# Scores in plain float32 in the quarters of the array, keys in blocks of 128, and eps added on ScalarE

## The chip, the core and the metric

The kernel runs on one core of a Trainium2 chip. TensorE (PE) multiplies; its weight loads have a row of their own in the profile (PEld). VectorE (DVE), ScalarE (ACT) and GpSimd (POOL) do the elementwise work, SyncE (SP) and POOL issue most transfers. The metric is the device time of one execution in microseconds (us).

## The reference

Attention with mixing over heads before and after the softmax, then two gated feed-forward layers, all in float32:

```python
scores = scale * np.matmul(q, k.transpose(0, 1, 3, 2))      # 2 batches, 12 heads, 448 x 448
scores = np.einsum('bhij,hg->bgij', scores, w_pre)
scores = scores - np.max(scores, axis=-1, keepdims=True)
attn = np.exp(scores)
attn = attn / (np.sum(attn, axis=-1, keepdims=True) + 1e-09)
attn = np.einsum('bhij,hg->bgij', attn, w_post)
x = np.matmul(attn, v)                                      # head_dim 64; then 896 x 768
x = (x @ w_a) * (x @ w_b) @ w_out                           # 768 -> 1536 -> 768
h = np.maximum(x @ w_in, 0.0)
out = (h * h) @ w_out2                                      # 768 -> 2048 -> 768
```

## The kernel before

The attention goes over eight tiles: batch b of 2, and four tiles t of query rows (120, 120, 120 and 88). A tile is cut into pairs of groups of ten rows: six pairs in a tile of 120, five in the tile of 88, 46 in all. One **slot** of the main loop does the following for one pair, and the order of all engines is fixed by the order of the calls in that loop:

- `premix` (L297): two groups of heads times `w_pre`, four float32 matmuls in the four 64x64 quarters of the array, out of G, the tile of scores with rows and heads on the partitions. Result in two of three PSUM banks "T".
- softmax: `smin` (a minimum on DVE, L306, into nb) and `sexp` (exponential on ACT with its sum, L313) for two halves; then `weights2` on DVE: z plus eps (L325), reciprocal (L326), and w2 = w_post / z (L327).
- `post` (L350): the exponentials e, 64 keys at a time, as stationary operand, and w2 (60 columns) as moving operand. This turns keys onto the partitions. The 448 keys are four blocks of 112, each cut in 64 and 48: 32 float32 matmuls for a pair, in quarters, into two PSUM banks "post" (from slot 38 on, in every other slot, "qk").
- `evac` copies both banks to A, the first on ACT (L377), the second on DVE (L375).
- `qk` (L212): scores of a later tile, for one pair of heads (six such calls for a tile), the heads in the two row halves of the array with up to 120 columns each, into two banks "qk". `qk_copy` takes them out, the even head on ACT (L223), the odd one on DVE (L221), and `spread` sends them by DMA to G (POOL issues for even heads, SP for odd ones). In batch 0, tiles 0 to 2, this is plain float32. From then on q and k are each split in a high and a low float32r part (`split_q`: ACT and six POOL subtractions, L170; `split_k`: ACT and DVE, L176 and L177), and three products are summed.

After the last slot of a tile comes `av` (L389): A times v, for each of six head pairs c four key blocks of 112 by two heads, each head in one column half of the array. The pairs go by two into a bank: c = 0, 1 into "av", c = 2, 3 into one of the two "post" banks, c = 4, 5 into "av" again; `av_out` (L399, DVE) copies each bank to x32. Between these calls stand the softmax of the pair after next, splits of k, and steps that split weights of the layers that follow (`steps`: ACT and DVE). In the text below T0 is the start of a tile's first `av` matmul.

The feed-forward layers follow the attention. They are 2448 float32r matmuls of 128x128 by 448 columns (L642 to L644).

Of the kernel before, what the change touches and what calls it, by code (L numbers as in the profile page):

```python
# [16 lines left out]
DM = H * D  # L17
# [11 lines left out]
JP = 112  # L29
NJ = S // JP  # L30
# [36 lines left out]
def place_mixed(g, k, h):  # L67
    return 64 * g + PK * (k % KG) + h


@with_exitstack
def attention_moe_kernel(
# [61 lines left out]
    kp = {}  # L134
    qp = {}
# [6 lines left out]
    def load_q(b, t, eng=nc.sync, parts=1):  # L142
        x = w_p.tile([128, UW], F32, tag="wc", name="q", bufs=2)
# [12 lines left out]
    def load_k(b, c, eng=nc.sync):  # L156
        if c % 3 == 0:
# [15 lines left out]
    def split_k(b, c):  # L173
        x = kk[b, c]
        hi, lo = single(f"ks{2 * c}"), single(f"ks{2 * c + 1}")
        nc.scalar.copy(hi, x)  # L176
        nc.vector.tensor_tensor(out=lo, in0=x, in1=rd(hi), op=ALU.subtract)  # L177
        kp[b, c] = (hi, lo)

    def split_q(b, t):  # L180
        n = NC * TILE
        x = qq[b, t]
        hi = w_p.tile([128, UW], F32R, tag="wh", name="qh", bufs=3)
        lo = w_p.tile([128, UW], F32R, tag="wl", name="ql", bufs=3)
        nc.scalar.copy(hi[:, 0:n], x[:, 0:n])
        lower(lo[:, 0:n], x[:, 0:n], hi[:, 0:n], 6)
        qp[b, t] = (hi, lo)

    def load_v(b, i, n=1):
        if b not in vv:  # L190
            x = sb.tile([128, NJ * DM], F32, tag="v", name="v", bufs=2)
            vv[b] = x[0:JP].rearrange("p (j d) -> p j d", j=NJ)
        g, j = divmod(i, NJ)
        nc.sync.dma_start(
            out=vv[b][:, j:j + n, g * DM // 2:(g + 1) * DM // 2], in_=v[b, g, j:j + n].rearrange("j p d -> p j d")
        )


    def qk(b, t, c, tags=("qk", "qk")):
# [108 lines left out]
    def sexp(b, m, f):  # L308
# [8 lines left out]
        E[b, m, f] = e  # L317

    def weights2(b, m):
# [5 lines left out]
        nc.vector.tensor_tensor(out=z, in0=z, in1=eps[0:q].to_broadcast([q, 2]), op=ALU.add)  # L325
# [12 lines left out]
    def post(b, m):  # L338
# [17 lines left out]
    def evac(b, m, g):  # L356
        t, r, n = PAIRS[m]
        if r == 0 and g == 0:
            A[b, t] = a_p.tile([JP, NJ * H, TILE], F32, tag="a", name="a")
        if g >= n:  # L360
            return
        src = Pps[b, m][g][0:JP, 0:2 * NJ * H * KG].rearrange("p (f g k) -> p f g k", f=2, k=KG)
# [16 lines left out]

    def av(b, t, c):  # L380
        n = ROWS[t]
        if c % 2 == 0:
            AVp[b, t] = ps("post" if c == 2 else "av")
        p = AVp[b, t]
        o = (c % 2) * TILE
        for j in range(NJ):
            for e in range(2):
                g = 2 * c + e
                nc.tensor.matmul(  # L389
                    p[64 * e:64 * e + 64, o:o + n], vv[b][:, j, g * D:(g + 1) * D], A[b, t][:, j * H + g, 0:n],  # L390
                    start=(j == 0), stop=(j == NJ - 1), skip_group_check=True,
                )

    def av_out(b, t, q):
        n = ROWS[t]
        if t == 0:
            x32[b][q] = xpair(b, q, F32)
        pv = AVp[b, t][:, 0:2 * TILE].rearrange("p (c i) -> p c i", c=2)
        nc.vector.tensor_copy(x32[b][q][:, :, OFFS[t]:OFFS[t] + n], pv[:, :, 0:n])  # L399
# [28 lines left out]
    v0 = sb.tile([128, NJ * DM], F32, tag="v", name="v0", bufs=2)  # L428
# [40 lines left out]
    def load_w(u, i=0, n=1):  # L469
# [20 lines left out]
    SPLITS = (  # L490
        (((0, 0), (0, 1), (0, 2)), (), ((0, 3),)),
        (((0, 4), (0, 5), (1, 0)), (), ((1, 1), (1, 2))),
        (((1, 3),), (), ((1, 4), (1, 5))),
    )
# [23 lines left out]
    for i in range(NJ):  # L518
        at(mid, 2, load_v, 0, 2 * i, 2)
    for ti, (b, t) in enumerate(tiles):  # L520
        s0, sp = base[ti], span[ti]
        if ti + 1 < len(tiles):
# [12 lines left out]
            if ti + 2 < len(tiles):  # L535
                if ti:
                    d = 3 if ti == 5 else 0
                    at(mid, s0 - 1 - d, load_q, *tiles[ti + 2], nc.sync, 2)
                    if not d:
                        at(mid, s0 + (ti != 3), split_q, *tiles[ti + 2])  # L540
        if ti + 1 < len(tiles):
            sl = s0 + sp - 1
            if ti == 4:
                at(end, sl, split_q, 1, 3)
            for c in range(NC):
                at(end, sl, av, b, t, c)
                if c % 2:
                    work = [(steps, STEPS[b, t][c // 2])] if (b, t) in STEPS else [
                        (split_k, *x) for x in SPLITS[t][c // 2]
                    ]  # L550
                    if c < 5:
                        for x in work:
                            at(end, sl, *x)
# [371 lines left out]
```

## Time and profile before

| | |
|---|---|
| median of 3 runs | 705.17 us (703.37 to 710.95) |
| the profiled execution: time, span | 704.41 us, 702.6 us |
| PE, PEld busy | 682.6 us (97%), 579.0 us (82%) |
| DVE, ACT, POOL busy | 489.1 us, 309.8 us, 67.5 us |
| attention, until the last av ends | 0 to about 204.4 us |
| feed-forward layers | about 204.4 to 702.6 us |

Matmuls are pipelined, and a record's length contains its way through the array. What a block of matmuls costs PE is therefore read from the start of its first record to the start of the next block. A float32 matmul leaves two records. An engine takes its instructions in the program's order, so an instruction that waits holds all that stand behind it.

### The profile page before, as it was taken

What the parts mean: (1) busy time and instruction counts of PE and PEld (TensorE: products, weight loads), DVE (VectorE), ACT (ScalarE), POOL (GpSimd) and SP (SyncE); (2) the same over time, 40 slices, a digit from 0 to 9 for tenths busy, and PEclk for the clock granted to TensorE, in tenths of its full rate; (3) what the DMA queues carried; (4) which work ended last, traced back from release to release, by engine and by line L of the source; (5) the groups of instructions that cost most, each with busy time, mean ns of one, the idle gap of its engine ahead of it and who ended that gap; (6) DMA issues with size and microseconds to landing.
All of it is one profiled execution on the core that took longest, in us unless ns stands there. A gap on an engine that the chain in (4) does not pass through costs nothing.

```text
span 702.6 us, 15964 instructions
## 1 busy us (share of the span) xinstructions
PE 682.6 (97%) x6749; PEld 579.0 (82%) x6749; DVE 489.1 (70%) x839; ACT 309.8 (44%) x580; POOL 67.5 (10%) x129
## 2 busy tenths in 40 slices
PE   9979998999899999999999999999999999999997
PEld 3445666666689999999999999999999999999996
DVE  6848987899865876766767556668888887645530
ACT  3647666777643333433333322335555553323210
POOL 7203331336200000000000000000000000000000
PEclk9989999999999999999999999999999999999999
DMA  7874576644202423332233422422324234343300
GB/s 232 207 194 140 163 193 178 175 121 145 86 3 90 135 90 113 113 124 102 90 121 104 135 90 90 135 90 96 130 90 132 94 96 153 137 147 130 117 28 27
DMA packets 29109, 84.94 MB, mean 121 GB/s; under 512 B 5075, under 2 KB 18478, under 8 KB 29037
## 3 DMA queue, kind: packets, MB, share of 16 engines
q1 hardware_dynamic: 23949, 73.24, 32.4%
q0 software_dynamic: 4224, 9.43, 5.3%
q8 instruction: 53, 0.87, 0.5%
q10 hardware_dynamic: 864, 1.24, 0.5%
q14 instruction: 19, 0.16, 0.1%
HBM read 62.29 MB, written 2.75 MB: 93 GB/s over the span
## 4 chain that ended last, share of the span: by engine, by line
PE 87%; DMA 5%; DVE 3%; issue 3%; ACT 2%; POOL 0%; ACTq 0%; DVEq 0%; POOLq 0%
PE T L642 9%; PE T L644 9%; PE T L643 9%; PE post L644 6%; PE post L643 6%; PE post L642 6%; PE qk L644 6%; PE qk L643 6%; PE qk L642 6%; PE post L350 4%; PE qk L212 4%; PE av L644 3%; PE av L643 3%; PE av L642 3%; PE av L389 3%
## 5 line engine op out<-in xcount | busy, mean ns | idle before, releaser
L604 ACT CAST wh<-wc 128x768 fp32r<-128x768 f32 x68 | 56.8, 835 | 118.2 <-DVE wc L598 104.6
L608 DVE TENSOR_TENSOR wl<-wc,wh 128x768 fp32r<-128x768 f32 x68 | 64.9, 954 | 48.2 <-ACT wh L604 48.1
L313 ACT ACTIVATE e<-T,nb 128x448 f32<-128x448 f32 (+1 forms) x92 | 57.6, 630 | 46.1 <-DVE nb L306 43.4
L644 PE MATMUL T<-m,wl 128*128 128x448 f32 x207 | 75.6, 365 | 0.0
L643 PE MATMUL T<-m,wh 128*128 128x448 f32 x207 | 75.6, 365 | 0.0
L642 PE MATMUL T<-m,wh 128*128 128x448 f32 x207 | 75.6, 365 | 0.0
L586 DVE SCALAR_TENSOR_TENSOR wa<-wr,wa 128x768 uint32<-128x768 uint32 x68 | 65.2, 958 | 2.3
L598 DVE SCALAR_TENSOR_TENSOR wc<-wc,wa 128x768 uint32<-128x768 uint32 x68 | 65.2, 958 | 2.3
L350 PEld LDWEIGHTS post<-w,e 64*48 64x48 f32 (+1 forms) x2624 | 44.0, 129 | 23.1 <-issue 11.1
L581 ACT ACTIVATE wc<-wr 128x768 f32<-128x768 f32 x68 | 61.3, 902 | 0.0
L306 DVE TENSOR_REDUCE nb<-T 128x1 f32<-128x448 f32 (+1 forms) x92 | 52.9, 615 | 7.5 <-PE T L297 6.3
L297 PE MATMUL T<-G,wpre_sb 64*64 64x448 f32 x352 | 49.7, 566 | 6.5 <-DMA G<-x 4.8
L350 PE MATMUL post<-w,e 64*48 64x60 f32 (+1 forms) x2624 | 49.9, 221 | 4.7 <-DVE w L327 2.5
L594 DVE TENSOR_SCALAR wc<-wc 128x768 f32<-128x768 f32 x68 | 38.0, 558 | 19.5 <-ACT wc L581 19.5
L642 PE MATMUL post<-m,wh 128*128 128x448 f32 x125 | 45.7, 365 | 0.0
L644 PE MATMUL post<-m,wl 128*128 128x448 f32 x125 | 45.6, 365 | 0.0
L643 PE MATMUL post<-m,wh 128*128 128x448 f32 x125 | 45.6, 365 | 0.0
L642 PE MATMUL qk<-m,wh 128*128 128x448 f32 x116 | 42.4, 365 | 0.0
L644 PE MATMUL qk<-m,wl 128*128 128x448 f32 x116 | 42.4, 365 | 0.0
L643 PE MATMUL qk<-m,wh 128*128 128x448 f32 x116 | 42.4, 365 | 0.0
L642 PEld LDWEIGHTS T<-m,wh 128*128 128x128 f32 x207 | 38.9, 188 | 3.1
L643 PEld LDWEIGHTS T<-m,wh 128*128 128x128 f32 x207 | 38.9, 188 | 3.1
(179 smaller groups left out, 1441.1 us busy)
## 6 DMA issues: line engine op xcount, KB each, us to landing
wr<-w SPq DMA_DIRECT2D x65, 768.0 KB
G<-s POOLq DMA_DIRECT2D x24, 210.0 KB, 5.2
G<-s SPq DMA_DIRECT2D x20, 210.0 KB
outT<-ta SPq DMA_DIRECT2D x11, 224.0 KB
wr<-w SPq DMA_DIRECT2D x12, 192.0 KB
k<-kT SPq DMA_DIRECT2D x9, 224.0 KB
q<-qT SPq DMA_DIRECT2D x10, 180.0 KB
G<-s POOLq DMA_DIRECT2D x12, 140.0 KB, 3.4
```

What stands on the lines that cost most here:

```text
L297: nc.tensor.matmul(p[f][o:o + 64, 0:S], wpre_sb[i:i + 64, o:o + 64], G[t % 2][i:i + 64, r + g, :], start=True, stop=True, skip_group_check ...
L306: nc.vector.tensor_reduce(out=NB[b, m][0:q, f:f + 1], in_=Tps[b, m][f][0:q, 0:S], op=ALU.min, axis=AX.X)
L313: nc.scalar.activation(out=e[0:q], in_=Tps[b, m][f][0:q, 0:S], func=ACTF.Exp, bias=NB[b, m][0:q, f:f + 1], scale=-1.0, accum_out=Z[b, m][0 ...
L350: nc.tensor.matmul(p[g][x:y, c:c + k], e[o:o + 64, j * JP + x:j * JP + y], w2[o:o + 64, f, :], start=True, stop=True, skip_group_check=True,)
L581: nc.scalar.activation(out=st["c"], in_=rd(st["high"]), func=ACTF.Abs, scale=HSC)
L586: nc.vector.scalar_tensor_tensor(out=a, in0=st["high"], scalar=0x80000000, in1=a, op0=ALU.bitwise_and, op1=ALU.bitwise_or)
L598: nc.vector.scalar_tensor_tensor(out=cu, in0=cu, scalar=3, in1=st["a"], op0=ALU.logical_shift_left, op1=ALU.bitwise_or)
L604: nc.scalar.copy(st["hi"], st["c"])
L608: nc.vector.tensor_tensor(out=lo, in0=st["c"], in1=rd(st["hi"]), op=ALU.subtract)
L642: nc.tensor.matmul(p[:, 0:S], hi[:, sl], x[0], start=first, stop=False)
L643: nc.tensor.matmul(p[:, 0:S], hi[:, sl], x[1], start=False, stop=False)
L644: nc.tensor.matmul(p[:, 0:S], lo[:, sl], x[0], start=False, stop=last)
```

## The change

- `qk`: plain float32 in all tiles. Each head pair is four matmuls in the four quarters: rows of q 0 to 63 and 64 to 119 in the column halves, the two heads in the row halves. `split_q` and `split_k` and their calls go. q gets buffers of its own, and the k of batch 1 goes straight to the tiles that held its parts.
- Keys: three blocks of 128 and a rest of 64. In `post` every stationary block has 64 columns; for the rest, the two column halves take half of the heads each, so their moving operand has 30 columns. Still 32 matmuls for a pair. A has 42 instead of 48 columns of (block, head) for a row; PSUM holds 420 instead of 480 values for a row of `evac`.
- `av`: `av_start` does the rest of 64 keys for all twelve heads, twelve matmuls in quarters, into **two** banks at once ("av" and "post"), which both stay in use to the end of the tile's `av`. Then c goes 0, 1, 4, 2, 3, 5 with three blocks of 128. `av_out` comes twice; each time DVE copies two head pairs (L414) and then ACT the third (L415).
- eps: `sexp` adds it on ACT (L315) behind the second exponential, instead of DVE in `weights2`.

```diff
     def qk(b, t, c, tags=("qk", "qk")):
...
-        if b == 0 and t < 3:
-            parts = [(qq[b, t], kk[b, c])]
-        else:
-            (qh, ql), (kh, kl) = qp[b, t], kp[b, c]
-            parts = [(qh, kh), (qh, kl), (ql, kh)]
-        for i, (x, y) in enumerate(parts):
+        for l, r in ((0, 64), (64, n)):
             for e in range(2):
                 o = 64 * e
                 nc.tensor.matmul(
-                    p[e][0:n, 0:S], x[o:o + 64, c * w:c * w + n], y[o:o + 64, :],
-                    start=(i == 0), stop=(i == len(parts) - 1),
+                    p[e][l:r, 0:S], qq[b, t][o:o + 64, c * w + l:c * w + r], kk[b, c][o:o + 64, :],
+                    start=True, stop=True, skip_group_check=True,
                 )
...
         E[b, m, f] = e
+        if f:
+            z = Z[b, m][0:q]
+            nc.scalar.activation(out=z, in_=z, func=ACTF.Identity, bias=eps[0:q])
...
-        nc.vector.tensor_tensor(out=z, in0=z, in1=eps[0:q].to_broadcast([q, 2]), op=ALU.add)
         nc.vector.reciprocal(out=z, in_=z)
...
-            for j in range(NJ):
+            for j in range(NK + 1):
                 for g in range(n):
                     o = 64 * g
-                    c = (f * NJ + j) * k
-                    for x, y in ((0, 64), (64, JP)):
+                    c = f * NG * KG + j * k
+                    for x in range(2):
+                        y, z, i = (64 * x, 0, k) if j < NK else (0, x * k // 2, k // 2)
                         nc.tensor.matmul(
-                            p[g][x:y, c:c + k], e[o:o + 64, j * JP + x:j * JP + y], w2[o:o + 64, f, :],
+                            p[g][64 * x:64 * x + 64, c:c + i],
+                            e[o:o + 64, j * 128 + y:j * 128 + y + 64], w2[o:o + 64, f, z:z + i],
...
+    def av_start(b, t):
+        n = ROWS[t]
+        AVp[b, t] = [ps(tag) for tag in ("av", "post")]
+        for two in ((0, 2), (1, 3), (4, 5)):
+            for e in range(2):
+                for c in two:
+                    x = 64 * side(2 * c + e)
+                    i, o = PLACE[c]
+                    nc.tensor.matmul(
+                        AVp[b, t][i][64 * e:64 * e + 64, o * TILE:o * TILE + n],
+                        vv[b][x:x + 64, 0, c * D:(c + 1) * D], A[b, t][x:x + 64, NK * H + c, 0:n],
+                        start=(o == 0), stop=False, skip_group_check=True,
+                    )
...
+        nc.vector.tensor_copy(x32[b][i][:, :, o], src[:, :, 0:n])
+        nc.scalar.copy(x32[b][2][:, i, o], p[:, 2 * TILE:2 * TILE + n])
...
-            for c in range(NC):
+            work = [[(steps, k)] for k in STEPS.get((b, t), (0, 0, 0))]
+            at(end, sl, av_start, b, t)
+            for i, c in enumerate(AVC):
                 at(end, sl, av, b, t, c)
...
+                if i == 1:
+                    at(end, sl, *work[0][0])
+                if i == 2:
+                    at(end, sl, av_out, b, t, 0)
+                    at(end, sl, softmax, sl + 2)
+                if i == 4:
+                    at(end, sl, *work[1][0])
+                    at(end, sl, weights2, *plist[sl + 2])
+            at(end, sl, av_out, b, t, 1)
+            at(end, sl, *work[2][0])
```

What moves on the engines is shown at three places. The first is DVE behind the last slot of tile (1, 2), whose `av` starts at 182.88 us in the trace: L399 and L414 are `av_out`, L306 and L301 the two minima of the softmax of the pair after next, L326/L327 and L323/L324 its `weights2`, the others steps on weights. Before:

```order
L327 TENSOR_TENSOR w_3533<-wp,z 128x120 [waits DVE_49]
L582 TENSOR_SCALAR wa<-wr 128x768 [waits DMAHW4_49,DMAHW3_49,DMAHW2_49]
L586 SCALAR_TENSOR_TENSOR wa<-wr,wa 128x768 [waits DVE_49]
L399 COPY x_0_2597<-av 128x2x120 [waits PE_49]
L306 TENSOR_REDUCE nb<-T 128x1 x2
L594 TENSOR_SCALAR wc<-wc 128x768 [waits Activation_49]
L399 COPY x_1_2624<-post 128x2x120 [waits PE_49]
L325 TENSOR_TENSOR z<-z,eps 128x2 [waits Activation_49]
L326 RECIPROCAL z<-z 128x2 [waits DVE_49]
L327 TENSOR_TENSOR w_3595<-wp,z 128x120 [waits DVE_49]
L399 COPY x_2_2647<-av 128x2x120 [waits PE_49]
L598 SCALAR_TENSOR_TENSOR wc<-wc,wa 128x768
```

The same place on DVE in the changed kernel:

```order
L324 TENSOR_TENSOR w_3420<-wp,z 128x120 [waits DVE_49]
L585 TENSOR_SCALAR wa<-wr 128x768 [waits DMAHW3_49,DMAHW2_49,DMAHW1_49]
L589 SCALAR_TENSOR_TENSOR wa<-wr,wa 128x768 [waits DVE_49]
L414 COPY x_0_2516<-av 128x2x120 [waits PE_49]
L301 TENSOR_REDUCE nb<-T 128x1 x2
L597 TENSOR_SCALAR wc<-wc 128x768 [waits Activation_49]
L323 RECIPROCAL z<-z 128x2 [waits Activation_49]
L324 TENSOR_TENSOR w_3492<-wp,z 128x120 [waits DVE_49]
L414 COPY x_1_2517<-post 128x2x120 [waits PE_49]
L601 SCALAR_TENSOR_TENSOR wc<-wc,wa 128x768
```

The copy out of "post" stood ahead of the `weights2` of the pair after next, and now stands behind it. On ACT the same stretch of the changed kernel reads as follows (L308 are the exponentials, L315 eps, L415 the third copy of `av_out`, L376 `evac`):

```order
L415 COPY x_2_2518<-av 128x120 [waits DVE_49]
L308 ACTIVATE e,z<-T,nb 128x448 [waits DVE_49] x2
L315 ACTIVATE z<-z,eps 128x2 [waits Activation_49]
L415 COPY x_2_2518<-post 128x120 [waits DVE_49]
L376 COPY a<-post 128x2x42x5 [waits PE_49]
```

There was no `av_out` on ACT before; each of the two copies waits for the copy that DVE makes of the same bank. The second place is PE behind the same `av`, in the changed kernel:

```order
L400 MATMUL av<-a,v 64x120 x18
L400 MATMUL post<-a,v 64x120 x18
L348 MATMUL post<-w_3420,e 64x60 [waits DVE_49]
L348 MATMUL post<-w_3420,e 64x60
L348 MATMUL post<-w_3420,e 64x60 [waits Activation_49]
```

The third matmul of `post` writes the bank that `av` used, and waits for ACT: for the second L415. (In the other tiles a `qk`, L207, stands between L400 and L348.) The third place is ACT in a slot in the midst of a tile. Before:

```order
L313 ACTIVATE e,z<-T,nb 128x448 [waits DVE_49]
L223 COPY s<-qk 120x448 [waits DMASW0_49,PE_49]
L377 COPY a<-post 112x2x48x5 [waits PE_49]
L185 CAST qh<-q 128x720 [waits DMAHW7_49,DMAHW6_49]
```

The same slot in the changed kernel:

```order
L308 ACTIVATE e,z<-T,nb 128x448 [waits DVE_49] x2
L315 ACTIVATE z<-z,eps 128x2 [waits Activation_49]
L218 COPY s<-qk 120x448 [waits DMASW0_49,PE_49]
L376 COPY a<-post 128x2x42x5 [waits PE_49]
```

The addition of eps stands between the second exponential and the copy that frees a "qk" bank; the cast of q is gone.

## Rows read from the trace of the kernel before

**Rows 1.** Windows; columns: window, length, busy of PE, PEld, DVE, ACT, POOL, PE clock, DMA share, GB/s.

```profile
45.00:200.60 155.60, 146.49 (x3710) 101.84 (x3702) 132.17 (x319) 107.29 (x261) 48.52 (x99) 1.00 0.51 143
204.40:702.60 498.20, 493.97 (x2438) 457.40 (x2436) 326.37 (x458) 182.49 (x272) 0.00 (x0) 1.00 0.31 106
```

**Rows 2.** Timeline, PE, unhindered blocks; columns: start, us, engine, line, operation, tiles, tile, count.

```profile
101.18 0.98 PE L297 MATMUL T<-G,wpre_sb 64*64 64x448 f32 x8
102.09 0.67 PE L212 MATMUL qk<-ks,qh 64*120 64x448 f32 x4
102.89 1.15 PE L350 MATMUL post<-w,e 64*64 64x60 f32 x64
103.87 0.99 PE L297 MATMUL T<-G,wpre_sb 64*64 64x448 f32 x8
```

**Rows 3.** Timeline, PE, a plain float32 qk and the block after it.

```profile
54.87 1.02 PE L212 MATMUL qk<-k,q 64*120 64x448 f32 x4
55.81 1.09 PE L350 MATMUL post<-w,e 64*64 64x60 f32 x62
```

**Rows 4.** Timeline of two slots in tile (1, 0), all engines.

```profile
149.83 1.15 DVE L306 TENSOR_REDUCE nb<-T 128x1 f32<-128x448 f32 x2
...
151.69 0.20 ACT L313 ACTIVATION_READ_ACCUMULATOR e<-T,nb 128x1 f32 x1
151.78 0.53 ACT L223 COPY s<-qk 120x448 f32<-120x448 f32 x1
...
153.13 1.15 PE L350 MATMUL post<-w,e 64*64 64x60 f32 x64
...
154.38 0.69 DVE L375 COPY a<-post 112x480 f32<-112x480 f32 x1
...
154.97 0.14 DVE L325 TENSOR_TENSOR z<-z,eps 128x2 f32<-128x2 f32 x1
...
155.14 0.17 DVE L326 RECIPROCAL z<-z 128x2 f32<-128x2 f32 x1
155.34 0.28 DVE L327 TENSOR_TENSOR w<-wp,z 128x120 f32<-128x120 f32 x1
155.54 0.62 DVE L306 TENSOR_REDUCE nb<-T 128x1 f32<-128x448 f32 x1
```

**Rows 5.** Timeline around the av of tile (0, 2), all engines.

```profile
93.15 1.86 PE L389 MATMUL av<-a,v 112*64 112x120 f32 x32 [0.17 <-DVE a L375]
...
94.81 1.84 PE L389 MATMUL post<-a,v 112*64 112x120 f32 x32
95.05 0.41 DVE L399 COPY x<-av 128x240 f32<-128x240 f32 x1
...
95.37 1.15 DVE L306 TENSOR_REDUCE nb<-T 128x1 f32<-128x448 f32 x2
96.10 0.63 ACT L313 ACTIVATE e<-T,nb 128x448 f32<-128x448 f32 x1 [1.70 <-DVE nb L306]
...
99.02 1.15 PE L350 MATMUL post<-w,e 64*64 64x60 f32 x64
```

**Rows 6.** Timeline around the av of tile (1, 2), all engines.

```profile
182.88 1.86 PE L389 MATMUL av<-a,v 112*64 112x120 f32 x32
...
187.95 1.09 PE L350 MATMUL post<-w,e 64*64 64x60 f32 x62
...
188.84 0.58 PE L297 MATMUL T<-G,wpre_sb 64*64 64x448 f32 x2
...
189.63 0.57 PE L350 MATMUL qk<-w,e 64*48 64x60 f32 x26
...
189.92 0.62 DVE L306 TENSOR_REDUCE nb<-T 128x1 f32<-128x448 f32 x1
```

**Rows 7.** DVE line L325: count, shortest, median and longest in ns.

```profile
L325 DVE TENSOR_TENSOR z<-z,eps x46: 138/152/1247, 17.6 to 197.4; 128x2 f32<-128x2 f32 x44, 64x2 f32<-64x2 f32 x2
```

**Rows 8.** Timeline around 82 us, POOL and DVE.

```profile
81.75 2.43 POOL L170 TENSOR_TENSOR ql<-q,qh 128x120 fp32r<-128x120 f32 x6
...
82.96 1.25 DVE L325 TENSOR_TENSOR z<-z,eps 128x2 f32<-128x2 f32 x1
```

**Rows 9.** Timeline, PE, the longest wait of the start.

```profile
40.36 1.95 PE L297 MATMUL T<-G,wpre_sb 64*64 64x448 f32 x8 [4.58 <-DMA G<-x]
```

**Rows 10.** Groups by form: copies out of PSUM on DVE and ACT; busy us, mean ns, idle before.

```profile
L375 DVE COPY a<-post 112x480 f32<-112x480 f32 x40 | 27.2, 681 | 12.0 <-PE post L350 11.6
L399 DVE COPY x<-av 128x240 f32<-128x240 f32 x12 | 4.8, 401 | 0.0
L371 ACT COPY a<-post 112x240 f32<-112x240 f32 x2 | 0.9, 434 | 2.0 <-PE post L350 2.0
```

More of the change, by code (lines that the diff above doesn't have):

```diff
@@ L28 @@
 GP = 128
-JP = 112
-NJ = S // JP
+NK = S // 128
+KH = S - 128 * NK
+NG = (NK * 2 + 1) * H // 2
+VP = 2 * NK + 1
 NC = DM // 128
@@ L133, in attention_moe_kernel @@
     kw = {}
-    kp = {}
-    qp = {}
     qq = {}
@@ L377, in evac, with av_out @@
             nc.scalar.copy(dst, src)
+    def av_start(b, t):
[11 more added lines that the diff above has]
+                    )
     def av(b, t, c):
         n = ROWS[t]
[L382 to L386, printed above, removed]
+        i, o = PLACE[c]
+        for j in range(NK):
             for e in range(2):
-                g = 2 * c + e
+                h = 2 * c + e
+                g, x = divmod(h, H // 2)
                 nc.tensor.matmul(
-                    p[64 * e:64 * e + 64, o:o + n], vv[b][:, j, g * D:(g + 1) * D], A[b, t][:, j * H + g, 0:n],
-                    start=(j == 0), stop=(j == NJ - 1), skip_group_check=True,
+                    AVp[b, t][i][64 * e:64 * e + 64, o * TILE:o * TILE + n],
+                    vv[b][:, 1 + NK * g + j, x * D:(x + 1) * D], A[b, t][:, j * H + column(h), 0:n],
+                    start=False, stop=(j == NK - 1), skip_group_check=True,
                 )
-    def av_out(b, t, q):
+    def av_out(b, t, i):
         n = ROWS[t]
[L396 to L399, printed above, removed]
+        if t == 0 and i == 0:
+            for q in range(NC // 2):
+                x32[b][q] = xpair(b, q, F32)
+        p = AVp[b, t][i]
+        o = slice(OFFS[t], OFFS[t] + n)
+        src = p[:, 0:2 * TILE].rearrange("p (c i) -> p c i", c=2)
+        nc.vector.tensor_copy(x32[b][i][:, :, o], src[:, :, 0:n])
+        nc.scalar.copy(x32[b][2][:, i, o], p[:, 2 * TILE:2 * TILE + n])
     warm = const.tile([128, 1], F16, name="warm")
@@ L516, in at @@
         d.setdefault(max(slot, 0), []).append(f)
-    for i in range(NJ):
-        at(mid, 2, load_v, 0, 2 * i, 2)
+    for i in range(0, VP, 2):
+        at(mid, 2, load_v, 0, i, 2)
     for ti, (b, t) in enumerate(tiles):
@@ L536, in attention_moe_kernel @@
                 if ti:
[L537 to L540, printed above, removed]
+                    at(mid, s0 - 1, load_q, *tiles[ti + 2], nc.sync, 2)
         if ti + 1 < len(tiles):
             sl = s0 + sp - 1
-            if ti == 4:
-                at(end, sl, split_q, 1, 3)
-            for c in range(NC):
+            work = [[(steps, k)] for k in STEPS.get((b, t), (0, 0, 0))]
+            at(end, sl, av_start, b, t)
+            for i, c in enumerate(AVC):
                 at(end, sl, av, b, t, c)
[L547 to L553, printed above, removed]
-                    at(end, sl, av_out, b, t, c // 2)
-                    if c == 5:
-                        for x in work:
-                            at(end, sl, *x)
-                    elif c == 3:
-                        at(end, sl, weights2, *plist[sl + 2])
-                    else:
-                        at(end, sl, softmax, sl + 2)
+                if i == 1:
[8 more added lines that the diff above has]
+            at(end, sl, *work[2][0])
         if ti == 2:
@@ L688, in attention_tail @@
         last = (B - 1, NTL - 1)
-        for c in range(NC):
+        av_start(*last)
+        for i, c in enumerate(AVC):
             av(*last, c)
-            if c % 2:
-                av_out(*last, c // 2)
+            if i % 3 == 2:
+                av_out(*last, i // 3)
+            if i % 2:
                 steps(1)
@@ L883, in _layout @@
     kT = k.reshape(B, NC, 2, S, D).transpose(0, 1, 2, 4, 3).reshape(B, NC, 128, S)
-    vl = v.reshape(B, 2, H // 2, NJ, JP, D).transpose(0, 1, 3, 4, 2, 5).reshape(B, 2, NJ, JP, DM // 2)
+    vl = np.zeros((B, VP, 128, H // 2, D), f)
+    n = NK * 128
+    vl[:, 1:] = v[:, :, 0:n].reshape(B, 2, H // 2, NK, 128, D).transpose(0, 1, 3, 4, 2, 5).reshape(vl[:, 1:].shape)
+    for h in range(H):
+        o = KH * side(h)
+        vl[:, 0, o:o + KH, h // 2] = v[:, h, n:]
+    vl = vl.reshape(B, VP, 128, DM // 2)
     wpre = np.zeros((128, 256), f)
@@ L890, in _layout @@
             wpre[np.ix_([place(n, h) for h in range(H)], o)] = i["w_pre"]
-            wpost[o, :, n % KG] = i["w_post"]
+            wpost[np.ix_(o, [column(h) for h in range(H)], [n % KG])] = i["w_post"][:, :, None]
         o = 128 + 64 * (n // KG)
```

51 lines of the change are left out of this document (21 added, 30 removed).

## The prediction

> **What bounds the kernel now.** I read the windows first, then the timeline of PE, then all engines over one slot and over one `av`. Behind 204.4 us PE is busy 494.0 of 498.2 us at the full granted clock (1.00 in the row, its 2.4 GHz level) [rows 1]. The change touches nothing there except when that stage starts. So the question is how long the attention takes. Between 45.0 and 200.6 us PE looks busy too, 146.5 of 155.6 us, but a record's length contains waits and the way through the array; block starts tell more.
>
> An unhindered split `qk` costs PE 0.80 us (102.09 to 102.89), a `post` 0.98, a `premix` 0.91 [rows 2]: 2.69 us for a slot. The slots in tile (1, 0) take 2.86 (two of them from 149.83 to 155.54) [rows 4]. What closes that circle is a loop over two slots: from the start of the minima to the start of the ACT copy of the even scores 1.95 us, the copy 0.53 (to 152.31; the "qk" bank is free only then), from there to `post` 0.82, to `evac` 1.25, to z 0.59, to the reciprocal 0.17, w2 0.20, and the next minimum 0.20, in all 5.71 [rows 4]. PE waits about 0.15 us a slot in it. So a gain on PE alone goes into that wait, and what counts is what the change does to this loop and to the `av` stretches.
>
> **The change part by part.**
>
> *A steady slot: 0.* Off the loop comes the addition on DVE, 0.17 (154.97 to 155.14) [rows 4], and in `evac` 60 of 480 columns: by the copies of 480 and 240 columns (681 and 401 ns) [rows 10] 1.17 ns each, 0.07. Onto it comes eps on ACT ahead of the copy that frees the bank. No row shows this operation. Its nearest row is the reading of the accumulator, which takes 0.20 but lets the next start after 0.09 (151.69, 151.78) [rows 4]. As eps waits for that reading to end, I take 0.11 for the wait and 0.11 for itself, 0.22. Bounds are 0.09 in all (no wait seen) and 0.11 + 0.32 = 0.43 (copies of 240 and 448 columns take 0.43 [rows 10] and 0.53 us [rows 4], so a copy of next to none 0.32). `qk` from the free bank to `post` was 0.82. In quarters it is what `premix` costs if the same array shape follows, 0.79 (188.84 to 189.63) [rows 6], plus at most one exposed weight load of about 0.05: 0 to +0.02. Sum -0.02 over two slots: nothing. With the bounds it is -0.07 to +0.1 a slot; some 26 slots run in this loop, so -1.8 to +2.6 us.
>
> *`post`: 0.* Its 64 records in four quarters take 0.98 us, 61 ns each in a quarter [rows 2]. A float32 `av` record of 120 columns takes 104 ns in a half (32 records in 1.66 us, 93.15 to 94.81) [rows 5], so 60 columns alone would take 52. The records with 64 stationary columns are thus held by something other than the columns that stream, and the count of records and their 64 columns stay. Making a quarter of them shorter gains nothing; if columns did count it is 1/8 of 0.8, 0.1 us a pair, half of it in the loop: 0 to -2 us, and I take 0.
>
> *`av` and what stands behind it: +4.9.* On PE: `av_start` is three matmuls in each quarter, 6 records of 104 ns, 0.62, plus about 0.15 for the first load and the change of array shape; the rest 36 records, 3.74. So it ends at T0 + 4.5; before, with `qk` after it, `post` came at T0 + 5.87 (93.15 to 99.02) [rows 5], without at T0 + 5.07 [rows 6]. PE could be at `post` by 5.4, or 4.6.
> But `post` needs both "post" banks, and one is now `av`'s to the end. Its release is the last link of a chain in order on DVE and ACT: c = 0, 1, 4 done at T0 + 0.77 + 1.87, seen by DVE 0.24 later (94.81 to 95.05) [rows 5]: first `av_out` at 2.9; minima 0.32 later, 3.2; exponentials 0.73 after that, 3.95 (95.05, 95.37, 96.10) [rows 5]; to the end of the second sum 1.34 (two starts 0.62 apart, each with its 0.52 and the 0.20 of the reading), 5.3; eps 0.2; reciprocal and w2 0.4, 5.9; second `av_out` 0.40, 6.3; then ACT's copy, which waits for DVE's, 0.3; `post` goes on at about T0 + 6.7. So it starts 0.8 us later than before in the six tiles of which this `post` follows a `qk`, and 1.6 later in tile (1, 2). In the tile of 88 rows PE shrinks with the rows, by 1.33 in the old order, the chain only by 0.7 in its first links: 1.4.
> How much is passed on? Behind 187.95 the next minimum starts 1.97 later [rows 6] and nothing else holds it: T0 + 8.65 against 7.04, all 1.6. Likewise the tile of 88 rows, of which I take 1.3. In the other five DVE comes later than PE today, with splits of k (which go) or steps on weights (which stay) in its queue: 0 to 0.8 each, I take 0.4. Sum 1.6 + 1.3 + 2.0 = 4.9, with bounds 2.5 and 7.
> The tile after which the feed-forward layers follow has no such `post`; there PE's 0.3 is gained in full.
>
> *What goes from POOL and ACT: -1.1.* The addition z + eps took 1247 ns once, against a median of 152 [rows 7], while POOL subtracted for `split_q` [rows 8]; PE's `post` waited for it. Both are gone: -1.1. POOL's 2.4 us for a tile also stood ahead of spreads, and some of the 2.4 may come back: 0 to -2. The casts and splits of k lie in `av` and are in the term above.
>
> *The start: -0.8.* The plain `qk` of batch 0 falls from 0.94 (54.87 to 55.81) [rows 3] to 0.8. But the first tile ends in a wait of 4.58 us for the scores of the next [rows 9], and engines wait there for transfers, so only an earlier issue can help: 0 to -1.5. I take 0.5, and 0.3 for the few plain slots behind that wait. Earlier starts of `av`, by 0.065 for the smaller `evac`, eight times: -0.5.
>
> **Sum** against the profiled execution's 704.4: + 4.9 - 1.1 - 0.8 - 0.5 - 0.3 = 706.6 us, 0.2% above the median of the runs (705.17, itself 0.8 above that execution).
>
> **A rule against the row.** A `premix` followed by `qk` in 64x120 tiles takes 0.91 [rows 2], one followed by a block in its own 64x64 shape 0.79 [rows 6]: 0.12 for the change of shape. The Trainium skill, TensorEngine Tiling (Array Packing), Key Properties, says that changing the tiling mode drains the array; by that rule a slot sheds this drain twice, and the trace agrees. What it would be worth if PE were the bound is the first rival.
>
> **The rivals.**
>
> 1. *PE's gains reach the end.* For: PE is busy at 97% by the page. Per slot with `qk` the premix falls by 0.12 (some 42 of them, 5.0 us), the 12 plain `qk` that follow the first six from 0.94 to 0.8 (1.7), `av` by 0.55 in six tiles and 0.35 in two (4.0): 10.7 in all, and -1.1 from POOL: 692.6. Against: PE waits in the loop of rows 4 already, and the held bank. It would show as slots below 2.7 us.
> 2. *The two row halves take turns in `av_start`* (slower). Both halves write both banks there at once; `premix`, `post` and `qk` keep each row half to a bank, so no row shows it. If they take turns, its 0.62 us doubles, DVE's chain starts 0.6 later, and all of it is passed on in eight tiles: 706.6 + 4.7 = 711.3. It decides the sign by the 1% bound from 0.7 us a tile upward (5.6 over eight tiles). The same page of the Trainium skill, PSUM Pressure, says that different row tiles cannot access the same PSUM bank simultaneously; by that rule this rival holds. No run here shows it so far.
> 3. *The waits behind `av` are absorbed.* If the softmax run ahead covers them, 4.9 becomes 0 to 1 and the time 702 to 703: still within 1%.
>
> **Chances.** Forecast with rival 3: 0.60 (700 to 711). Rival 1, whole or in half: 0.24 (690 to 698). Rival 2 or deeper waits behind `av`: 0.16 (709 to 716). One per cent is 7 us, about what a measurement of this kernel can tell from no change. Faster by over 1% is below 698.1: most of rival 1 and a little of the forecast, 0.24. Slower is above 712.2: half of rival 2 and an edge of the forecast's, 0.13. The rest 0.63. The range is 695.5 to 713: it reaches halfway into rival 1 and over most of rival 2, and holds the bounds above. The forecast's own is 700 to 711.
>
> **What would show each step.** In the changed profile, a slot in tile (1, 0) at 2.8 to 2.9 us, with eps on ACT at 0.1 to 0.25 us; `post` still at 0.98; `qk` plus `premix` without the 0.12; `av` of 4.5 us (5.1 if rows take turns); and behind it PE waiting 1.0 to 2.0 us in `post` for ACT's L415. If that wait is missing, or slots fall below 2.7, the forecast is wrong in that term.

## The result, and the profile after

The changed kernel takes 709.91 us (median of 20 runs, 706.72 to 714.18), the kernel before 703.07 (20 runs beside them, 699.78 to 710.95). The ratio is 1.0103, with a 95% interval of 1.0082 to 1.0123: slower by 1.0%. The forecast was 706.6, no change by the 1% bound; its range of 695.5 to 713.0 holds the time. The profiled execution has a span of 706.0 us, against 702.6 before: these two executions differ by 3.4 us, the medians by 6.8. Runs of an experiment that fell into a slower state of the chip (one of `epsdve`, one of `q56post`, two of `q56eps`, two of the kernel before beside `qkonly`) are left out of the medians below.

First, where the time is not. A window of the changed kernel, with the columns of [rows 1]:

```profile
207.75:705.95 498.20, 493.97 (x2438) 457.52 (x2436) 326.28 (x457) 182.83 (x273) 0.00 (x0) 1.00 0.31 106
```

The feed-forward stage has the same length (498.20 us) and the same busy time of PE (493.97) as in [rows 1]. It only starts 3.35 us later, at 207.75 in place of 204.4. So all is decided in the attention. There the starts of the minima (the first of each pair, a pair being one slot) tell where time is gained and lost. Those of the ninth and of the last pair on DVE, first the kernel before, then the changed one:

```profile
54.99 1.16 DVE L306 TENSOR_REDUCE nb<-T 128x1 f32<-128x448 f32 x2
...
195.29 1.14 DVE L306 TENSOR_REDUCE nb<-T 64x1 f32<-64x448 f32 x2
```

```profile
48.99 1.16 DVE L301 TENSOR_REDUCE nb<-T 128x1 f32<-128x448 f32 x2 [0.16 <-PE T L292]
...
198.83 1.14 DVE L301 TENSOR_REDUCE nb<-T 64x1 f32<-64x448 f32 x2
```

The changed kernel is 6.0 us ahead at the ninth pair, 4.1 ahead at the start of the slow slots of tile (1, 1) (the 34th pair, 148.66 against 152.74), level at the 39th (171.98 against 172.17), and 3.5 behind at the last. (The slots between the `av` of tile (1, 0) and that of (1, 1) are those of tile (1, 1). [rows 4], the prediction and the expectations call them slots of tile (1, 0); their times are right.) A large gain at the start, which the prediction had at 0.8, is lost again, and more. The next rows show the place where most of it goes. PE and its weight loads (PEld) in the changed kernel, first an ordinary `qk` of a tile with 120 rows, then one of tile (1, 3), which has 88:

```profile
142.61 0.29 PEld L207 LDWEIGHTS qk<-ks,q 64*64 64x64 f32 x7 [0.18 <-DVE s L216]
142.67 1.02 PE L207 MATMUL qk<-ks,q 64*64 64x448 f32 x8
...
143.42 1.10 PE L348 MATMUL post<-w,e 64*64 64x60 f32 x60
...
151.26 0.96 PE L292 MATMUL T<-G,wpre_sb 64*64 64x448 f32 x8
...
152.04 1.79 PE L207 MATMUL qk<-ks,q 64*64 64x448 f32 x8
152.04 0.15 PEld L207 LDWEIGHTS qk<-ks,q 64*64 64x64 f32 x2 [0.23 <-issue]
152.89 0.13 PEld L207 LDWEIGHTS qk<-ks,q 64*24 64x24 f32 x4 [0.70 <-issue]
153.76 1.13 PE L348 MATMUL post<-w,e 64*64 64x60 f32 x64
```

Start to start, the ordinary `qk` costs 0.75 us (142.67 to 143.42): its four quarters run beside one another, and its loads follow in one go. The other costs 1.72 (152.04 to 153.76). Its quarters of 64 columns go first; the loads of the quarters of 24 columns come only 0.85 later, when those are done, and the second half runs by itself. 88 rows are 64 + 24 columns, 120 are 64 + 56. By the rows of line L207 there are 48 records of 64*24, four (two matmuls) in each of 12 `qk`:

```profile
L207 PE MATMUL qk<-ks,q x192: 536/536/587, 80.6 to 172.8; 64*64 64x448 f32 x96, 64*56 64x448 f32 x72, 64*24 64x448 f32 x24
L207 PE MATMUL qk<-k,q x160: 536/536/1004, 4.6 to 78.4; 64*64 64x448 f32 x80, 64*56 64x448 f32 x44, 64*24 64x448 f32 x24, 64*36 64x448 f32 x12
```

The second place is the one that the prediction named. PE, DVE and ACT in and behind the `av` of tile (1, 0), which starts at 134.33, in the changed kernel (the 24 records of `av_start` ahead of it, the weight loads, and the rows of DVE and ACT that have no part in it are left out):

```profile
135.10 2.07 PE L400 MATMUL av<-a,v 128*64 128x120 f32 x36
137.00 2.02 PE L400 MATMUL post<-a,v 128*64 128x120 f32 x36
137.22 0.41 DVE L414 COPY x<-av 128x240 f32<-128x240 f32 x1 [0.21 <-PE av L400]
138.94 0.98 PE L207 MATMUL qk<-ks,q 64*64 64x448 f32 x8
139.75 0.28 PE L348 MATMUL post<-w,e 64*64 64x60 f32 x4
140.29 0.40 DVE L414 COPY x<-post 128x240 f32<-128x240 f32 x1
140.73 0.26 ACT L415 COPY x<-post 128x120 f32<-128x120 f32 x1 [0.87 <-DVE x L414]
141.04 1.03 PE L348 MATMUL post<-w,e 64*64 64x60 f32 x56 [1.02 <-ACT x L415]
```

`av` takes 4.61 us (134.33 to 138.94). Then `post` leaves four records (two matmuls) and stands until ACT has copied the last of the bank, and goes on at T0 + 6.71; the prediction had 6.7. All seven stretches, T0 being the start of `av`, with the first minimum of the second pair that DVE reaches behind T0:

| behind the `av` of | (0,0) | (0,1) | (0,2) | (0,3) | (1,0) | (1,1) | (1,2) |
|---|---|---|---|---|---|---|---|
| before, second pair at T0 + | 7.98 | 8.40 | 9.25 | 6.66 | 8.32 | 8.00 | 7.04 |
| after | 8.66 | 8.67 | 9.75 | 7.86 | 8.66 | 8.66 | 10.19 |
| start to start over the wait in `post` | 1.23 | 0.22 | 1.23 | 1.55 | 1.23 | 0.22 | 1.99 |

In (0, 1) and (1, 1) a `qk` with 24 columns stands between `av` and `post` and covers the wait. In (1, 2) something more comes on top. PE, and below it windows of the changed kernel (columns as in [rows 1]):

```profile
187.74 0.33 PE L348 MATMUL post<-w,e 64*64 64x60 f32 x4
189.83 1.77 PE L348 MATMUL post<-w,e 64*64 64x60 f32 x57 [1.77 <-ACT x L415]
...
188.00:190.00 2.00, 0.23 (x11) 0.17 (x11) 1.28 (x4) 0.88 (x4) 0.00 (x0) 0.98 0.47 187
190.00:192.00 2.00, 2.00 (x64) 1.80 (x65) 0.59 (x2) 0.37 (x1) 0.00 (x0) 0.50 0.00 0
```

Behind the wait the granted clock stands at 0.50, the 1.2 GHz level, and `post` and `premix` take twice as long: the next minimum comes at T0 + 10.19 and not at the predicted 8.65.

### The profile page after: what moved, and what is told of

Read it like the earlier page. It is cut to its first block, busy times and chain, and to the rows that moved or that the text cites. A ratio compares the mean times of both kernels' runs of the same rounds, so it can differ in the third digit from the quotient of the medians.

```text
span 706.0 us, 16098 instructions
## 1 busy us (share of the span) xinstructions
PE 685.6 (97%) x6881; PEld 579.2 (82%) x6881; DVE 471.4 (67%) x773; ACT 314.9 (45%) x625; POOL 54.5 (8%) x99
## 3 DMA queue, kind: packets, MB, share of 16 engines
HBM read 62.29 MB, written 2.75 MB: 92 GB/s over the span
## 4 chain that ended last, share of the span: by engine, by line
PE 89%; DMA 3%; ACT 3%; DVE 2%; issue 1%; SPq 1%; POOL 0%; DVEq 0%; ACTq 0%; POOLq 0%
PE T L645 9%; PE T L647 9%; PE T L646 9%; PE post L646 6%; PE post L647 6%; PE post L645 6%; PE qk L647 6%; PE qk L645 6%; PE qk L646 6%; PE post L348 5%; PE qk L207 5%; PE T L292 4%; PE av L647 3%; PE av L646 3%; PE av L645 3%; PE av L400 2%
## 5 line engine op out<-in xcount | busy, mean ns | idle before, releaser
L348 PEld LDWEIGHTS post<-w,e 64*64 64x64 f32 x2624 | 52.0, 136 | 29.3 <-issue 9.2
L308 ACT ACTIVATE e<-T,nb 128x448 f32<-128x448 f32 (+1 forms) x92 | 57.7, 631 | 30.8 <-DVE nb L301 30.8
L348 PE MATMUL post<-w,e 64*64 64x60 f32 (+1 forms) x2624 | 54.7, 220 | 8.8 <-ACT x L415 6.2
L301 DVE TENSOR_REDUCE nb<-T 128x1 f32<-128x448 f32 (+1 forms) x92 | 53.0, 617 | 7.7 <-PE T L292 6.4
L645 PEld LDWEIGHTS T<-m,wh 128*128 128x128 f32 x207 | 38.9, 188 | 3.1
L647 PEld LDWEIGHTS T<-m,wl 128*128 128x128 f32 x207 | 38.9, 188 | 3.1
```

Source lines behind the costliest of these rows:

```text
L301: nc.vector.tensor_reduce(out=NB[b, m][0:q, f:f + 1], in_=Tps[b, m][f][0:q, 0:S], op=ALU.min, axis=AX.X)
L308: nc.scalar.activation(out=e[0:q], in_=Tps[b, m][f][0:q, 0:S], func=ACTF.Exp, bias=NB[b, m][0:q, f:f + 1], scale=-1.0, accum_out=Z[b, m][0 ...
L348: nc.tensor.matmul(p[g][64 * x:64 * x + 64, c:c + i], e[o:o + 64, j * 128 + y:j * 128 + y + 64], w2[o:o + 64, f, z:z + i], start=True, sto ...
L645: nc.tensor.matmul(p[:, 0:S], hi[:, sl], x[0], start=first, stop=False)
L647: nc.tensor.matmul(p[:, 0:S], lo[:, sl], x[0], start=False, stop=last)
```

## The experiments

Two theories stood against each other. **A (shape):** the narrow quarters of the 88-row tiles cost the time. **B (held bank):** the bank that `av` holds costs more than the 4.9 us of the sum. All ratios below are to the kernel before.

**56 columns in every second range** (`q56`), A alone:

```diff
-        n = ROWS[t] if b + t else ROWS0
+        n = TILE if b + t else ROWS0
```

> The changed kernel, with one edit: in the tiles of 88 rows the second column range of qk takes the 32 zero columns behind the 24 real ones too, so its quarters have 56 stationary columns as in every other tile; the 32 rows of scores that this adds are never read. Theory A (shape): the two quarters with 24 columns do not run beside those with 64; in the changed kernel's trace a qk of the tiles (0, 3) and (1, 3) takes 1.72 us from its start to the next block, one of the other tiles 0.75. By A all twelve fall to 0.75 to 0.80, the slots of tile (1, 0) behind 148 us from 3.8 to 2.8 or 2.9 us, and the time falls by 4 to 8 us from 709.9, to about 704. Theory B (held bank): the loss lies behind the av stretches, where post waits for the bank that av holds; by B these qk cost only slack, the time moves by less than 1.5 us, and the waits for L415 stay.

Measured: 702.69 us (12 runs), ratio 0.9996 (0.9974 to 1.0018), 7.2 below the changed kernel. The `qk` of tile (1, 3) takes 0.75, and the slot of the 34th pair falls from 3.77 us (148.66 to 152.43) to 2.75 (144.63 to 147.38). The `qk` and the `post` behind it:

```profile
150.28 1.08 PE L207 MATMUL qk<-ks,q 64*64 64x448 f32 x8
151.03 1.10 PE L348 MATMUL post<-w,e 64*64 64x60 f32 x56
```

The 12 narrow `qk` cost PE some 0.95 each, 11.4 us in all, of which 7.2 reach the end. This one edit undoes the whole slowdown, though the waits for L415 are now there in all seven stretches. A holds; B cannot be the main cause.

**The post bank first** (`postfirst`):

```diff
-        AVp[b, t] = [ps(tag) for tag in ("av", "post")]
+        AVp[b, t] = [ps(tag) for tag in ("post", "av")]
```

> The changed kernel, with one edit: av fills the post bank first and the av bank second, so that the bank that post waits for is copied out after 18 of the 36 av records of a pass, and the copy that comes last is of the bank that nobody waits for. Theory B (held bank): the waits of 1.0 to 2.0 us in post for L415 go, in tile (1, 2) the drop of the granted clock to its 1.2 GHz level behind the wait goes with it, and the first minimum there comes at T0 + 6.7 to 7.1 in place of T0 + 10.2; the time falls by 4 to 7 us from 709.9, to about 704. Theory A (shape): the waits go too, but behind the av of (0, 1) and (1, 1), where a qk with 24 columns stands, nothing changes, and the time falls by 3 to 5. Rival (absorbed): the softmax that runs ahead had covered the waits, and the time moves by less than 2.

Measured: 707.94 us (10 runs), ratio 1.0078 (1.0046 to 1.0110), 2.0 below the changed kernel, with intervals that overlap. In its trace the waits for L415 are gone, and the second pair behind the `av` of (1, 2) comes at T0 + 7.66. By those minima 5.3 us should have gone; the profiled execution gave part of them back in another wait (3.4 us from start to start at 107 us, named issue), behind which the granted clock stands at 0.50 from 110 to 116. That is below the 3 to 5 of A and the 4 to 7 of B, and at the edge of the third case (absorbed, less than 2): the wait exists, but is worth about 2, which these runs do not tell from nothing.

**eps on DVE** (`epsdve`):

```diff
-            nc.scalar.activation(out=z, in_=z, func=ACTF.Identity, bias=eps[0:q])
+        nc.vector.tensor_tensor(out=z, in0=z, in1=eps[0:q].to_broadcast([q, 2]), op=ALU.add)
```

> The changed kernel, with eps added by DVE again, ahead of the reciprocal. On ACT eps moves the copy of the even scores from 0.09 us behind the start of the second accumulator reading to 0.43 behind it (0.34 later, where the prediction had 0.22, later than 0.09 by 0.13); on DVE it costs 0.17 ahead of the reciprocal. If this loop sets the slots, the time falls by 1 to 3 us from 709.9; if the slots are set by PE or by another engine, it moves by less than 1 us either way.

**All three** (`all3`):

> The changed kernel with all three edits: 56 columns in every second range of qk, the post bank filled and copied out first, eps on DVE. If the causes are apart from one another, the gains add: by A and B together 8 to 13 us from 709.9, to about 699, 3 to 6 us below the kernel before; if they cover one another, no more than the larger of them, about 704. By the first rival of the prediction (PE's gains reach the end) it should now come to about 693.

Measured: `epsdve` 708.41 (5 runs; ratio 1.0079, 1.0061 to 1.0098), 1.5 below the changed kernel and less than the two intervals can tell apart. `all3` 698.92 (6 runs), ratio 0.9930 (0.9903 to 0.9957): faster than both kernels, 11.0 below the changed one, and mostly the sum of the parts (7.2, 2.0 and 1.5). The 693 of the first rival is not reached.

**Where the price begins** (`q40`, `q32`). The edit is `q56` with another width, in the 88-row tiles alone:

```diff
-        for l, r in ((0, 64), (64, n)):
+        for l, r in ((0, 64), (64, 104 if n == 88 else n)):
```

(96 for 104 in `q32`.)

> The changed kernel; in the tiles of 88 rows the second range of qk takes 40 columns (24 real, 16 of the zero columns behind them, whose scores are never read). Theory A in its narrow form (the array's tile): a quarter of up to 32 columns is another tile of the array than one of 64, and 40 columns belong to the wide one; such a qk then takes 0.75 to 0.80 us, as with 56, and the time is that of 56 columns, about 703. Rival C (the count of columns): the price falls evenly from 1.72 us at 24 columns to 0.75 at 56, so 40 columns give about 1.24 us and a time of 706 to 707.

> The same with 32 columns (24 real, 8 zero). Theory A in its narrow form: as with 24 columns, 1.72 us for a qk of these tiles, and a time of about 710. Rival C: about 1.48 us, and a time of 708.

PEld and PE around one such `qk`, with 32 columns and then with 40:

```profile
155.23 0.15 PEld L207 LDWEIGHTS qk<-ks,q 64*64 64x64 f32 x2 [0.23 <-issue]
156.08 0.14 PEld L207 LDWEIGHTS qk<-ks,q 64*32 64x32 f32 x4 [0.71 <-issue]
155.23 1.80 PE L207 MATMUL qk<-ks,q 64*64 64x448 f32 x8
156.96 1.13 PE L348 MATMUL post<-w,e 64*64 64x60 f32 x64
```

```profile
158.21 0.66 PEld L207 LDWEIGHTS qk<-ks,q 64*64 64x64 f32 x8
158.59 1.08 PE L207 MATMUL qk<-ks,q 64*64 64x448 f32 x8
159.34 1.10 PE L348 MATMUL post<-w,e 64*64 64x60 f32 x56
```

32 columns cost 1.73 us like 24, 40 cost 0.75 like 56. It is a step between 32 and 40, and not a price per column: rival C is out. (The 36 columns of the first tile, in the forms above, belong to the wide side: 0.79 to 0.98 us in five of its six `qk`.) The Trainium skill, TensorEngine Tiling (Array Packing), Available Configurations, lists tiles of 64 rows by 64 columns and by 32 as two modes; with its Key Properties, by which a change of mode drains the engine, narrow and wide quarters could not share the array, and the trace agrees (the narrow loads come 0.85 us behind the wide ones). The times, 711.33 for 32 columns (2 runs; ratio 1.0121, 1.0086 to 1.0155) and 706.67 for 40 (3 runs; 1.0050, 1.0018 to 1.0081), are less sharp than the traces. The second was expected near 703 by A, and 706.67 is what rival C said; it is the `qk` of 0.75 us that speaks against C, not the time. The profiled execution of `q40` has waits of 2.9 and 2.4 us at 34 and 108 us, start to start, where that of `q56` has 1.7 and none, and its granted clock is at 0.50 behind both, where that of `q56` stays up. That this explains the 4.0 us between the two medians is not shown.

**56 columns and the post bank first** (`q56post`), eps still on ACT:

> The changed kernel with 56 columns in every second range of qk and the post bank filled and copied out first; eps stays on ACT. With the narrow quarters gone no slow qk covers the wait behind an av, so all seven waits for L415 (1.23 us in five tiles, 1.55 and 1.98 in the others, with 56 columns alone) should go. If what they cost reaches the end, the time falls by 4 to 6 us from the 702.7 of 56 columns alone, below the 698.9 of all three edits or level with it; if DVE's own queue behind the av holds the next minimum anyway, by 1.5 to 3, to about 700.5, and eps on DVE brings the rest of the 3.8 us between 702.7 and 698.9.

Measured: 700.02 us (11 runs), ratio 0.9976 (0.9952 to 1.0000), 2.7 below `q56`, by the ratios 1.4; the intervals overlap. Rows of the waits of PE (waited for, us in total, times, longest), in the changed kernel and in `q56`:

```profile
PE post L348 <- ACT x L415: 6.2, 5, 1.8
```

```profile
PE post L348 <- ACT x L415: 8.2, 7, 1.8
```

In `q56post` no such row is left, and still only some 2 of the 8.2 us come back, about the smaller of the two cases expected. A wait of `qk` for ACT's copies takes part of its place, which `q56` has not:

```profile
PE qk L207 <- ACT s L218: 1.8, 4, 0.6
```

**eps on DVE with 56 columns** (`q56eps`):

> The changed kernel with 56 columns in every second range of qk and eps on DVE; av still fills the av bank first. A slot in tile (1, 0) takes 2.81 us with eps on ACT (three of them in 8.42 us), 2.76 with eps on DVE in the kernel with all three edits: 0.05 a slot, over the some 26 slots of this loop 1.3 us, and 0.07 in each of the seven chains behind an av. So the time falls by 1 to 2 us from 702.7, to about 701; if slots elsewhere do not follow this loop, by less than 0.7.

Measured: 703.10 us (10 runs), ratio 0.9991 (0.9962 to 1.0020), no gain on the 702.69 of `q56`. Three slots of tile (1, 1), from the 32nd pair to the 35th, take 8.34 us with eps on DVE, 8.42 on ACT and 8.47 in the kernel before. Where eps stands does not matter here, as the sum had it.

**The scores alone** (`qkonly`): the kernel before with the new `qk` (56 columns), the buffer for q, k loaded where its split stood, and no splits; its main lines are

```diff
-        x = w_p.tile([128, UW], F32, tag="wc", name="q", bufs=2)
+        x = sb.tile([128, NC * TILE], F32, tag="q", name="q", bufs=2)
...
-    SPLITS = (
...
+    SPLITS = (((),) * 3,) * 3
```

> The kernel before, with one part of the change alone: scores in plain float32 in quarters of the array (56 columns in every second range), q in a buffer of its own, k loaded to where its split stood, no splits. Keys stay in four blocks of 112, av and eps as before. If the shorter start, the POOL work that goes and nothing else make up what the changed kernel gains, this has all of the gain and none of the losses: the first av starts at 40 to 44 us, no post waits behind an av, and the time is 697 to 700, level with all three edits (698.9); the new blocks of keys and the new av are then worth nothing. If the start came from the other sizes of v or from the new av, the first av starts at 46 to 48 and the time is 702 to 704.

Measured: 700.61 us (12 runs), ratio 0.9960 (0.9931 to 0.9989), a gain of 2.6 on the kernel before beside it (703.16). Its ninth pair starts at 49.90, against 54.99 before. So the gain of the start comes with the scores, not with the new keys. New keys, new `av` and eps together cost 2.1 more (`q56`, 702.69), and bring about 1.7 once the post bank is filled first and eps is back (`all3`, 698.92); both differences are within the intervals.

**The start: old qk in the first two tiles** (`startold`; `q56` with one range for the first two tiles):

```diff
-        for l, r in ((0, 64), (64, n)):
+        for l, r in (((0, n),) if b == 0 and t < 2 else ((0, 64), (64, n))):
```

> The changed kernel with 56 columns in every second range, but qk of the first two tiles of batch 0 in halves of the array over all their columns, as in the kernel before. The start up to the first av came out 4 to 6 us earlier in the changed kernels, where the prediction had 0.8. If the shorter qk of the start does it (each earlier by 0.15 us, so the scores go out earlier and the wait for the transfer into G, 4.58 us before, stays short and the granted clock up), the first av starts at 44 to 47 us again and the time rises by 3 to 5 us from 702.7. If something else does it (q in a buffer of its own, other sizes of v, chance in the DMA queues), the first av stays at 40 to 42 us and the time moves by less than 1.5.

Measured: 705.06 us, ratio 1.0029 (1.0006 to 1.0052), 2.4 above `q56`: between the two cases. In its trace the wait ahead of the seventh pair stays short (1.25 us from start to start) and `av` starts at 40.1, so the shorter `qk` does not shorten this wait; a wait named issue then takes 3.9 us in `av_start`, and the ninth pair starts at 53.76, later than with the short `qk` in any execution below. Whether that wait belongs to the longer `qk` or is a draw is undecided.

**Both kernels profiled again** (`before2`, `after2`):

> The kernel before, unchanged, profiled once more. In its first profile PE waited 4.58 us for the transfer into G at 40.36 us, the granted clock stood at its 1.2 GHz level from 40 to 45, and the first av began at 47.0 us; in the seven changed variants profiled so far that kept the short start it began at 40 to 44. If the long wait belongs to the kernel before, it comes again, the first av begins at 46 to 48 us, and the changed start is worth 3 to 6 us. If it was a draw of that one execution, the wait is 1 to 3 us, the first av begins at 41 to 45, and the start of the changed kernel is worth no more than the 0 to 1.5 us of the prediction.

> The changed kernel, unchanged, profiled once more. What belongs to it comes again: qk of the 88-row tiles 1.72 to 1.95 us, the waits of 1.23, 1.55 and 1.99 us for L415, the drop of the granted clock behind the av of tile (1, 2). What was a draw differs: the length of the wait for transfers at the start (first av at 40.3 us) and the place and length of waits that the profile calls issue (0.82 us at 38.3).

The profiled executions took 703.86 and 711.58 us. The 4.58 us of [rows 9] were a draw: here the same premix waits 1.13. But what that wins is lost at once. The kernel before, second execution, all engines:

```profile
36.81 1.17 PE L297 MATMUL T<-G,wpre_sb 64*64 64x448 f32 x8 [1.13 <-DMA v<-v]
...
44.24 0.53 ACT L223 COPY s<-qk 120x448 f32<-120x448 f32 x1 [2.93 <-DMA G<-s]
44.67 1.50 ACT L176 CAST ks<-k 128x448 fp32r<-128x448 f32 x3
...
45.27 1.70 DVE L177 TENSOR_TENSOR ks<-k,ks 128x448 fp32r<-128x448 f32 x3 [1.64 <-ACT ks L176]
46.88 0.40 DVE L399 COPY x<-av 128x240 f32<-128x240 f32 x1
...
47.33 3.47 PE L389 MATMUL av<-a,v 112*64 112x120 f32 x32 [1.92 <-DVE x L399]
...
54.96 1.16 DVE L306 TENSOR_REDUCE nb<-T 128x1 f32<-128x448 f32 x2
```

ACT waits for a transfer, the casts of k stand behind it, DVE's subtractions behind the casts, DVE's copy out of the "av" bank behind those, and `av` behind that copy. The ninth pair starts at 54.96, as in the first execution (54.99). In the changed kernel and its variants that keep the short `qk` it starts at 48.99 to 52.85 (eleven profiled executions, mean 50.6): 4.4 us earlier, where the sum had 0.8. So neither of the two cases expected holds whole: the wait was a draw, and the start is still worth more than 1.5.

Part of this goes with the granted clock. In both executions of the kernel before it falls to the 1.2 GHz level ahead of the ninth pair (a mean of 0.53 from 40 to 47 us in the first, and from 47 to 54 in the second). The 32 records of `av` above then take 3.47 us in place of the 1.86 of [rows 5]. A window of the second execution (columns as in [rows 1]):

```profile
47.00:54.00 7.00, 6.67 (x104) 5.06 (x108) 3.83 (x10) 2.33 (x6) 0.56 (x1) 0.53 0.21 64
```

Of the eleven executions, four have no such drop up to there (the first `after`, `q32`, `q56`, `q56post`), and their ninth pair starts at 48.99 to 50.33; in the seven others it starts at 49.59 to 52.85. How much of the 4.4 us is the clock and how much the splits is not shown.

What belongs to the changed kernel came again in `after2` (narrow `qk` of 1.72 and more, waits of 1.23, 1.55 and 1.98), but not the drop of the clock in (1, 2): there the second pair came at T0 + 8.66.

## Why the forecast failed, step by step

**The step that failed** is the term of the steady slot: "In quarters it is what `premix` costs if the same array shape follows, 0.79". That holds for six of the eight tiles. In the other two 88 rows leave a rest of 24 columns, another shape of the array, and the `qk` costs 1.72. The prediction shortened the chain behind `av` for the tile of 88 rows, and did not ask what its rows do to the quarters. It even weighed the price of a changed shape, between `premix` and `qk`, and not within `qk`. Nothing in [rows 1 to 10] shows a quarter of 24 columns; the bound "0 to +0.02" was set without a row for it. Missing from the sum: 7.2 us. No rival held this cause either. That the time lies in the range, and at the lower end of what rival 2 was given (709 to 716), is luck: rival 2 is not there (below), and the term that fills its place was not in the sum.

**The start** was mis-sized the other way: -0.8 predicted, with a bound of -1.5 for the first tile; -4.4 measured at the ninth pair. The prediction put the casts and splits of k into the `av` term and read the 4.58 of [rows 9] as a fixed wait for data. In the second execution the splits of k carried a late transfer on to `av`, and a lower clock came on top. That the splits also do it in the first, where the granted clock was low from 40 to 47 us, is not shown.

**The av stretches** were right in mechanism and size as far as DVE goes: `av` 4.61 (4.5 predicted), `post` at T0 + 6.71 (6.7), the second pair behind (1, 2) at T0 + 8.66 (8.65) where the clock stays up. Without the drop the delays in the table add up to 5.3, against 4.9. But undoing the wait brought back only 2.7 (`q56post`) and 2.0 (`postfirst`), neither clear of the noise. Some of it may have been absorbed later, as rival 3 had it; that is not shown.

**eps:** the operation was bigger than its bound of 0.1 to 0.25. Behind the second reading of the accumulator on ACT:

```profile
144.79 0.20 ACT L308 ACTIVATION_READ_ACCUMULATOR e<-T,nb 128x1 f32 x1
145.02 0.29 ACT L315 ACTIVATE z<-z,eps 128x2 f32<-128x2 f32 x1
145.22 0.51 ACT L218 COPY s<-qk 120x448 f32<-120x448 f32 x1
```

It takes 0.29 us, and the copy starts 0.43 behind the reading (145.22 less 144.79), where it started 0.09 behind it in [rows 4]: at the upper bound of the sum. The Trainium skill, ScalarE: Activation LUTs, Rules for kernel authors, gives about 0.3 us for each activation with a bias operand; the trace agrees. In the time it changes nothing that `q56eps` could show: the reciprocal no longer stands behind an addition, and the slot stays at 2.8.

**premix** falls from 0.91 to 0.78 (151.26 to 152.04) and `post` stays near its 0.98 (0.95), as forecast, without effect on slots of 2.8. **Rival 2** is out. The first records of `av_start` write both banks from both row halves a few ns apart, and the next four follow 0.1 us later:

```profile
134.33 0.28 PE L387 MATMUL av<-a,v 64*64 64x120 f32 x1
134.33 0.31 PE L387 MATMUL post<-a,v 64*64 64x120 f32 x1
134.34 0.31 PE L387 MATMUL av<-a,v 64*64 64x120 f32 x1
134.35 0.31 PE L387 MATMUL post<-a,v 64*64 64x120 f32 x1
134.45 0.26 PE L387 MATMUL av<-a,v 64*64 64x120 f32 x1
```

They take no turns: 0.77 us in all (134.33 to 135.10), as the sum had it (0.62 + 0.15). Here the measurement differs from the PSUM Pressure rule of the Trainium skill, TensorEngine Tiling (Array Packing), as that rival read it.

**The sum, corrected** by differences of medians: the scores with POOL's stall and the start -2.6 (`qkonly`; predicted -1.9), the rest of the change +2.1 (`q56` less `qkonly`; predicted +4.1), the narrow quarters +7.2 (predicted 0). These are steps from one kernel to the next, so that they add up to the measured 6.8 by construction, which proves nothing; what they show is the size of each step. The second is within the intervals, so neither it nor the first can be told from what was predicted. The third is far outside them. Without the narrow quarters the change would have been within 1%, as forecast (`q56`, 702.69).

## What to carry to other kernels

Before a block is split over tiles of the array, list the widths of the rest for every tile of the loop, the ragged ones too: here a rest of 24 or 32 columns beside 64-wide tiles more than doubled the block (1.72 us in place of 0.75), and one padded to 40 or 56 with zeros that nobody reads left it at 0.75. When a new accumulator borrows a bank that others wait for, fill and empty that bank first (here the waits went, and about 2 us with them, at the edge of the noise). A wait seen in one profiled execution is a draw until a second one shows it.

## What the hardware showed that was not expected

- **A step in width.** Four quarters of float32 with 448 moving columns: 1.72 to 1.73 us with 24 or 32 columns in the second pair, 0.75 with 40 or 56 (the shortest of the twelve of each kernel, start to start).
- **The clock after a short wait.** Behind the wait of about 2 us in `post` in tile (1, 2) the granted clock fell to 0.50 in three of the eight profiled executions that have this wait (the changed kernel's first, `q56`, `q40`), and stayed at 1.00 in five, `after2` among them. A drop moves the second pair from T0 + 8.66 to 9.95 and more.
- **Waits named issue.** PE stands in them at places that change from one execution to the next of the same kernel: 2.1 us at 107 us before; 0.8 at 38 us in the first profile of the changed kernel, 2.0 at 41 and 2.8 at 111 in its second (all from start to start). They may be part of the spread of 7.5 us over its 20 runs. What they wait for the profile doesn't show, and it stays open.
